# Issuing the loads of x for four pairs of chunks from GpSimd instead of SyncE, in a fused Mamba-2 and SwiGLU kernel

## The chip, the core and the metric

The kernel runs on one core of one Trainium2 chip. The core has five engines that run their own instruction streams: TensorE (PE in the profile, with its weight loads listed apart as PEld), VectorE (DVE), ScalarE (ACT), GpSimd (POOL) and SyncE (SP). SP does no arithmetic; it issues transfers between DRAM and the on-chip memory (DMAs). Sixteen DMA engines carry them out. An engine works through its own stream in order, so an instruction that waits holds up everything behind it on that engine.

The metric is the time of one execution on the device in microseconds. The kernel before takes 395.5 us, the median of 3 runs (395.0 to 396.29).

## The reference

Two stages follow one another. The first is a Mamba-2 scan in chunks, for 4 batches of 8 heads, 768 positions, a head width of 32 and a state of 16:

```python
for c in range(nc):
    la = log_a[:, :, sl]
    cum = np.cumsum(la, axis=-1)
    L = np.exp(cum[:, :, :, None] - cum[:, :, None, :]) * causal
    CB = np.einsum('bhin,bhjn->bhij', Cc, Bc)
    y_intra = np.einsum('bhij,bhjd->bhid', CB * L, xc)
    y_inter = np.einsum('bhin,bhnd->bhid', Cc, state) * np.exp(cum)[:, :, :, None]
    y[:, :, sl] = y_intra + y_inter
    Bx = np.einsum('bhjn,bhjd->bhjnd', Bc, xc) * decay_from_j[:, :, :, None, None]
    state = decay_full[:, :, None, None] * state + np.sum(Bx, axis=2)
```

The second takes the result as 3072 tokens of 256 features, divides each by its root mean square, and applies a SwiGLU layer with a hidden width of 1536:

```python
xn = x / rms * rms_g
g = xn @ w_gate
silu = g * (1.0 / (1.0 + np.exp(-g)))
val = xn @ w_val
out = silu * val @ w_out
```

x enters the scan in two places: as the factor of the masked matrix in `y_intra`, and in the additions to the state, `Bx`.

## The kernel before, in words

The kernel works on chunks of 128 positions, taken in twelve pairs: pair p holds chunks 2p and 2p + 1 of one batch. Two pairs make one block of 512 tokens for the second stage, so there are six blocks. The pairs are counted from 0 in what follows, so the third to sixth pairs are pairs 2 to 5. Blocks 1 to 5 compute the products with the gate and value weights (`product_gv`, L917 to L936, step `P.k.j`) by a scheme that needs seven products instead of eight for each 2 by 2 arrangement of submatrices; it works on sums and differences of weights, which `combine_w` (L893 to L904, steps `cw` on DVE and `cwp` on POOL) makes once, and of activations, which `combine_x` (L906 to L912, steps `tx` on DVE and `txp` on POOL) makes for each block. Block 0 uses it for the last three of its six columns, and plain products for the others (`products_gv` L849, `products_early` L859).

Before they can be used, the weights pass through a conversion: `fetch` (L153) loads a piece of a weight matrix into one of six buffers `wr`, `power` (ACT, L199), `mantissa` (DVE, L216 and L219) and `weight` (DVE, L225) turn it into the wanted numbers. This fills the first 95 us of DVE and ACT.

No scheduler decides the order. A string of steps at the end of the kernel is read from left to right, and each step emits its instructions on the engines that its function names. A word such as `0:x.2` calls the function that is listed under `x` in `first_kinds` for pair 2; the steps of the blocks 1 to 5 are looked up in `kinds` instead. The order of each engine's stream is thus the order of the words. Waits are put in for data and for buffers. A DMA is issued in the stream of the engine whose queue is named, at its place in that stream.

The loads of x are made by `load_x(p, queue)` (L127 to L132). It takes one of the three buffers `xr` and issues two DMAs, one for each chunk, each with 128 positions on the partitions and, for each position, 8 heads of 32 numbers: 1024 runs of 128 bytes, 128 KB. The step `x` in `settings` (L373) serves pairs 0 to 5, and the step `x` in `kinds` (L1247) serves pairs 6 to 11. With three buffers, pair 2 takes a fresh one, pairs 3 and 5 those of pairs 0 and 1, and pair 4 that of pair 2.

Around the four loads the order reads (cut, with only the words that are spoken of below):

```
0:sq.0 ... 0:y.1/2 0:sq.1 ... 0:xn.0 ... 0:dT.3 0:man.4 0:table.1 0:x.2 ... 0:gate.2/0 0:txp.0.0 0:cw.0.0
0:gg.2/1 ... 0:A.2 0:txp.0.1 0:silu.3 0:x.3 ... 0:tx.0.2 1:dT.0 1:table 0:txp.0.3 ... 0:cwp.3.0 ... 0:cw.4.0
... 0:y.2/2 0:S.3 0:x.5 0:cwp.4.1 ... 0:P.2.3 0:bc.4 0:x.4 ... 0:sq.2 ... 0:cwp.3.3 0:P.5.3 1:spread.0 0:cwp.1.0
0:P.7.3 0:P.6.4 0:P.5.4 0:P.4.3 0:hidgp.11.3 ... 0:cwp.4.2 0:cwp.4.3 ... 0:P.3.3 ... 0:cwp.5.0 ... 0:P.7.4 ... 0:y.3/2
```

The takers of x are: `A.2` (L648), the additions to the state for pair 2; `y.2` (L720), the outputs of pair 2, at whose end stand the additions for pair 3; and `y.3`, the outputs of pair 3, at whose end stand the additions for pairs 4 and 5. On POOL in this stretch are `sq` (L761 and L772, sums of squares), `txp`, `cwp` (written as `sw<-...` and `wgv<-wgv` in the profile, since one of the four combinations is made in place) and `hidgp` (L960, the product of the two halves of the hidden layer).

Of the kernel before, what the change touches and what calls it, by code (L numbers as in the profile page):

```python
# [20 lines left out]
def kernel(  # L21
# [33 lines left out]
    nc = tc.nc  # L55
# [71 lines left out]
    def load_x(p, queue=nc.sync):  # L127
        b, c0 = divmod(2 * p, NC)
        st.setdefault(p, {})["x"] = raw.tile([P, 2, NH, D], FP32, tag="xr", name="xr")
        for i in range(2):  # L130
            sl = slice((c0 + i) * P, (c0 + i + 1) * P)
            queue.dma_start(out=st[p]["x"][:, i], in_=x[b, :, sl, :].rearrange("h s n -> s h n"))  # L132
# [210 lines left out]
    def minus_mid():  # L343
# [26 lines left out]
        "log": lambda: activation(out=la, in_=la0, func=AF.Ln), "mids": minus_mid,  # L370
        "bc": lambda p: load(p, (nc.sync, nc.scalar) if p == 0 else (nc.sync,) * (1 if p == 1 else 2)),
        "bc2": load_chunk,
        "x": load_x,  # L373
    }


# [1082 lines left out]
```

## Time and profile before

| | |
|---|---|
| median of 3 runs | 395.5 us (395.0 to 396.29) |
| the profiled execution's own time | 395.41 us |
| its span, from the first to the last instruction | 393.7 us |
| granted TensorE clock | 1.00 |
| busy: PE, PEld | 386.9, 332.2 us |
| busy: DVE, ACT, POOL | 285.3, 234.1, 151.8 us |
| DMA: packets, of them under 512 bytes | 92533, 77416 |
| DMA: bytes moved | 27.01 MB |

The profile is of one execution, whose own time stands beside its span. Times in its rows are microseconds from the start of the span. A row of the order of time gives the start, the length, the engine, the line of the kernel, the operation, what it writes and reads, and how many instructions are merged into the row; brackets show how long the engine was idle before and what it waited for. SPq is SP's queue: its rows are the issues, not the transfers themselves. A transfer's landing is given as the time from its issue. Matmuls are pipelined and their ends are modelled, so that PE can show as busy without being at its peak. The DMA engines' share is the mean over all 16.

### The profile page before, as it was taken

To read this page: it belongs to the slowest core of one execution; us is meant where nothing else is said; L and a number is where in the kernel's file an instruction comes from. 1 tells how busy PE (TensorE), PEld (TensorE's weight loads), DVE (VectorE), ACT (ScalarE), POOL (GpSimd) and SP (SyncE) were. 2 spreads that over 40 slices of the span, in tenths; PEclk is the share of its full clock that TensorE was granted. 3 is DMA by queue.
4 is the path that set the end of the run, shared out by engine and by line. 5 is a ranking of instruction groups with operands and counts; after the bars stand their busy time and mean duration, and the time that the engine had idled before them with its cause. 6 is when DMAs were issued, how large, how long until landed. Compare 5 with 4: busy or idle time off the path is not lost.

```text
span 393.7 us, 9631 instructions
## 1 busy us (share of the span) xinstructions
PE 386.9 (98%) x3837; PEld 332.2 (84%) x3837; DVE 285.3 (72%) x594; ACT 234.1 (59%) x483; POOL 151.8 (39%) x170
## 2 busy tenths in 40 slices
PE   8999999999999999999999999999999999999996
PEld 5675478888888899888889888899888899988995
DVE  7999999997748967484897765676654587455574
ACT  3899889978599492447651544676345740555410
POOL 5022054454648378003563611466402155211271
PEclk9999999999999999999999999999999999999999
DMA  8988986682002538202423002000100000100001
GB/s 93 252 173 249 246 153 210 121 160 63 6 0 68 78 85 128 70 0 36 102 44 75 15 0 68 2 23 28 43 0 3 0 8 27 55 0 2 1 2 53
DMA packets 92533, 27.01 MB, mean 69 GB/s; under 512 B 77416, under 2 KB 86344, under 8 KB 92488
## 3 DMA queue, kind: packets, MB, share of 16 engines
q1 hardware_dynamic: 90408, 26.26, 29.8%
q8 instruction: 30, 0.49, 0.5%
q10 hardware_dynamic: 2080, 0.13, 0.4%
q14 instruction: 15, 0.12, 0.1%
HBM read 22.64 MB, written 3.74 MB: 67 GB/s over the span
## 4 chain that ended last, share of the span: by engine, by line
PE 81%; DVE 11%; issue 4%; ACT 3%; DVEq 0%; ACTq 0%
PE gate L935 27%; PE o L1056 21%; PE val L935 20%; PE o L967 4%; PE y L720 3%; PE g L583 1%; DVE wgv L225 1%; DVE m L219 1%; DVE m L216 1%; PE tp L533 1%; DVE hid L882 1%; PE g L576 1%; PE e L453 1%; PE y L648 1%; DVE S L672 1%
## 5 line engine op out<-in xcount | busy, mean ns | idle before, releaser
L947 DVE TENSOR_TENSOR c<-val,p 128x512 f32<-128x512 f32 x99 | 67.5, 687 | 40.3 <-PE val L935 28.3
L941 ACT COPY p<-gate 128x512 f32<-128x512 f32 x99 | 56.9, 584 | 58.0 <-PE gate L935 56.3
L960 POOL TENSOR_TENSOR hid<-c 128x256 f32<-128x256 f32 x41 | 34.0, 837 | 88.8 <-ACT c L197 82.6
L935 PE MATMUL gate<-tx,wgv 128*128 128x256 f32 x264 | 65.8, 382 | 0.0
L197 ACT ACTIVATE c<-c 128x256 f32<-128x256 f32 x99 | 39.3, 415 | 30.1 <-DVE c L947 29.6
L935 PEld LDWEIGHTS gate<-tx,wgv 128*128 128x128 f32 x264 | 49.0, 190 | 7.2 <-issue 0.3
L960 DVE TENSOR_TENSOR hid<-c 128x256 f32<-128x256 f32 x58 | 28.4, 498 | 17.0 <-ACT c L197 17.0
L1087 DVE TENSOR_TENSOR ob<-ob,o 128x128 f32<-128x128 f32 (+1 forms) x90 | 24.4, 299 | 20.7 <-PE o L1056 18.0
L1056 PE MATMUL o<-two,hid 128*128 128x128 f32 x280 | 36.2, 276 | 0.1
L1056 PEld LDWEIGHTS o<-two,hid 128*128 128x128 f32 x280 | 34.4, 192 | 1.1 <-issue 0.2
L935 PE MATMUL val<-tx,sw 128*128 128x256 f32 x132 | 34.0, 382 | 0.0
L935 PE MATMUL val<-xn,sw 128*128 128x256 f32 x132 | 33.7, 380 | 0.0
L935 PE MATMUL gate<-tx,sw 128*128 128x256 f32 x132 | 33.4, 381 | 0.0
L935 PE MATMUL gate<-xn,wgv 128*128 128x256 f32 x132 | 33.2, 381 | 0.2 <-DVE xn L831 0.2
L935 PE MATMUL val<-xn,wgv 128*128 128x256 f32 x132 | 33.3, 380 | 0.0
L486 POOL TENSOR_SCALAR_AFFINE_SELECT L<-L 64x512 f32<-64x512 f32 x32 | 23.0, 718 | 13.5 <-ACT L L197 10.9
L935 PEld LDWEIGHTS val<-tx,sw 128*128 128x128 f32 x132 | 24.7, 190 | 4.0 <-issue 0.4
L935 PEld LDWEIGHTS val<-xn,wgv 128*128 128x128 f32 x132 | 24.9, 190 | 3.4
L935 PEld LDWEIGHTS gate<-xn,wgv 128*128 128x128 f32 x132 | 24.4, 190 | 4.0 <-ACT e L197 0.6
L935 PEld LDWEIGHTS gate<-tx,sw 128*128 128x128 f32 x132 | 24.6, 190 | 3.4 <-issue 0.2
L197 ACT ACTIVATE u<-gate 128x256 f32<-128x256 f32 (+1 forms) x37 | 14.8, 402 | 21.2 <-PE gate L935 20.1
L935 PEld LDWEIGHTS val<-xn,sw 128*128 128x128 f32 x132 | 24.5, 190 | 3.2 <-issue 0.2
(199 smaller groups left out, 737.2 us busy)
## 6 DMA issues: line engine op xcount, KB each, us to landing
L<-rowd SPq DMA_DIRECT2D x32, 128.0 KB, 3.3
xr<-in_x_dram SPq DMA_DIRECT2D x24, 128.0 KB, 3.8
wr<-in_moe_w_out_dram SPq DMA_DIRECT2D x6, 512.0 KB, 3.6
out_dram<-ob SPq DMA_DIRECT2D x24, 128.0 KB, 1.7
wr<-in_moe_w_gate_dram SPq DMA_DIRECT2D x5, 512.0 KB, 6.3
wr<-in_moe_w_val_dram SPq DMA_DIRECT2D x5, 512.0 KB, 4.9
br<-in_B_dram SPq DMA_DIRECT2D x23, 64.0 KB, 2.9
cr<-in_C_dram SPq DMA_DIRECT2D x23, 64.0 KB, 2.9
```

Source lines behind the costliest of these rows:

```text
L197: nc.scalar.activation(**operands)
L216: nc.vector.tensor_scalar(out=m, in0=hi, scalar1=0xFFFFF, scalar2=0x100000, op0=ALU.bitwise_and, op1=ALU.bitwise_or)
L219: nc.vector.scalar_tensor_tensor(out=f, in0=lo.bitcast(U32), scalar=2.0 ** -32, in1=m, op0=ALU.mult, op1=ALU.add)
L486: nc.gpsimd.affine_select(out=L[r], in_=L[r], pattern=[[0, L.shape[1]], [1, HC]], compare_op=ALU.is_ge, fill=0.0, base=0, channel_multipli ...
L720: nc.tensor.matmul(out=y[2 * k + u][rows, (2 * n + i) * HC:(2 * n + i + 1) * HC], start=(k, u, rows.start) not in opened, stop=True, skip_ ...
L935: nc.tensor.matmul(out=dst[:, half[w]], lhsT=lhsT, rhs=rhs, start=(k in (1, 2, 5) and w == 0), stop=True, skip_group_check=True)
L941: nc.scalar.copy(out=t, in_=Xs[j])
L947: nc.vector.tensor_tensor(out=t, in0=Zs[j], in1=a, op=ALU.add)
L960: engine.tensor_tensor(out=hid[:, 2 * j + c // 10 - 1, c % 10 - 1], in0=u, in1=src[:, half[1]], op=ALU.mult)
L967: nc.tensor.matmul(out=o, lhsT=hid[:, f, k // 2, (k % 2) * P:(k % 2 + 1) * P], rhs=wo[:, f], start=opens, stop=(f == NF - 1), skip_group_c ...
L1056: nc.tensor.matmul(out=Os[blk, b][:, place * P:(place + 1) * P], lhsT=hidden_or_sum(u)[:, g], rhs=rhs, start=(blk, b) not in opened, stop= ...
L1087: nc.vector.tensor_tensor(out=o, in0=o, in1=src, op=ALU.add if what[0] == "+" else ALU.subtract)
```

## The change

The step `x` for the pairs 0 to 5 names the queue itself: SP for pairs 0 and 1, GpSimd for pairs 2, 3, 5 and 4, in this order. The words in the order string stay where they are. `load_x` is unchanged, and so is the step `x` of the later blocks.

```diff
-        "x": load_x,
+        "x": lambda p: load_x(p, nc.sync if p < 2 else nc.gpsimd),
```

By the order of the words, the eight issues leave SP's stream and enter POOL's: those of pair 2 stand between the second `sq` of L761 and `txp.0.0`, those of pair 3 between `txp.0.1` and `txp.0.3`, those of pair 5 between `cwp.3.0` and `cwp.4.1`, and those of pair 4 between `cwp.4.1` and the `sq` of pair 2. The streams of PE, DVE and ACT hold the same instructions in the same order. The waits of the eight DMAs on their buffers move with them.

## Prediction

> **What bounds the kernel now.** I read the page's totals and chain first, then the queue that the loads leave and the one they enter, then who takes what stands behind them.
>
> From the page: the busy times, the chain of work that ended last, and the loads in question.
>
> ```profile
> PE 386.9 (98%) x3837; PEld 332.2 (84%) x3837; DVE 285.3 (72%) x594; ACT 234.1 (59%) x483; POOL 151.8 (39%) x170
> ...
> PE 81%; DVE 11%; issue 4%; ACT 3%; DVEq 0%; ACTq 0%
> ...
> xr<-in_x_dram SPq DMA_DIRECT2D x24, 128.0 KB, 3.8
> ```
>
> PE is busy 386.9 of 393.7 us, so at most 6.8 us are left to win in the whole span, while whatever makes PE wait is added to the end. The granted clock is 1.00 in every stretch.
>
> The order of time on SP's queue shows the four pairs of loads as they go out now (start, length of the two):
>
> ```profile
> 32.34 1.08 SPq L132 DMA_DIRECT2D xr<-in_x_dram  x2
> ...
> 35.49 2.26 SPq L132 DMA_DIRECT2D xr<-in_x_dram  x2
> ...
> 48.97 2.09 SPq L132 DMA_DIRECT2D xr<-in_x_dram  x2
> ...
> 54.59 2.26 SPq L132 DMA_DIRECT2D xr<-in_x_dram  x2
> ```
>
> They are pairs 2, 3, 5 and 4 (counted from 0). Now POOL's own order of time; brackets give the idle time before and what ended it:
>
> ```profile
> 30.85 0.73 POOL L912 TENSOR_TENSOR tx<-xn 128x256 f32<-128x256 f32 x1 [7.51 <-DVE xn L835]
> 31.66 1.59 POOL L912 TENSOR_TENSOR tx<-xn,tx 128x256 f32<-128x256 f32 x2
> 49.68 1.12 POOL L904 TENSOR_TENSOR sw<-wgv 128x256 f32<-128x256 f32 x1 [16.43 <-DVE wgv L225]
> 52.95 0.73 POOL L904 TENSOR_TENSOR sw<-sw,wgv 128x256 f32<-128x256 f32 x1 [2.15 <-DVE sw L904]
> 55.10 0.73 POOL L772 TENSOR_TENSOR sq<-sq 128x256 f32<-128x256 f32 x1 [1.42 <-ACT sq L197]
> 55.79 0.74 POOL L904 TENSOR_TENSOR sw<-wgv,sw 128x256 f32<-128x256 f32 x1
> 56.48 0.74 POOL L904 TENSOR_TENSOR sw<-wgv 128x256 f32<-128x256 f32 x1
> 57.19 1.18 POOL L960 TENSOR_TENSOR hid<-c 128x256 f32<-128x256 f32 x1
> 58.33 0.90 POOL L904 TENSOR_TENSOR wgv<-wgv 128x256 f32<-128x256 f32 x1
> 59.20 0.73 POOL L904 TENSOR_TENSOR sw<-wgv,sw 128x256 f32<-128x256 f32 x1
> 62.23 0.87 POOL L904 TENSOR_TENSOR sw<-wgv 128x256 f32<-128x256 f32 x1 [2.29 <-DVE wgv L225]
> ```
>
> Two wide holes (7.51 and 16.43 us), two narrow ones (2.15 and 1.42), then a run without a gap from 55.10 to 59.93. What this run makes are weights for PE, and PE's weight loads say when each is taken:
>
> ```profile
> 57.32 0.84 PEld L935 LDWEIGHTS gate<-tx,sw 128*128 128x128 f32 x4
> ...
> 59.91 0.84 PEld L935 LDWEIGHTS val<-xn,sw 128*128 128x128 f32 x4
> 60.77 0.84 PEld L935 LDWEIGHTS gate<-tx,wgv 128*128 128x128 f32 x4
> ```
>
> The chain in order of time is PE alone from 55.08 to 63.79: a wait there is paid in full.
>
> **The change part by part.**
>
> *Taken from SP.* Eight issues, 1.08 + 2.26 + 2.09 + 2.26 = 7.7 us of its queue. The loads behind them (gate and value weights, dT, B and C, the rows for L) may go out up to that much sooner. I cost this at nothing: the weight loads wait for their buffers (SP waited 1.7 us for ACT's e and 3.9 us for DVE's m), and their takers do not wait: between 20 and 60 us DVE is 97% busy and its longest idle piece is 0.24 us. If that cover were gone, the gain would be bounded by PE's idle time between 50 and 60 us, 0.51 us.
>
> *Added to POOL.* Eight issues of 128 KB, each of 128 x 8 runs of 128 bytes. In program order pair 2 stands behind the second sq of L761 (done at 23.34), pair 3 between the second and third tx, pair 5 behind the first sw (50.80), pair 4 behind the second (53.68). Only pair 4 has a late release: it takes pair 2's buffer when y.2 is over at 49.9, so it does not wait either. Everything on POOL behind an issue waits for it.
>
> The trace has no DMA issued by POOL, so the price g of one issue is bounded. Below: SP's issue of the same load, 0.37 us at its shortest, 0.58 at the median. Above: one step of POOL's own two-input operation for every run, 731 ns / 256 = 2.85 ns, times 1024 = 2.9 us; with a step for each of the two ends of a run, 5.8 us. Between lies POOL's one-input operation, the affine select of L486, 718 ns / 512 = 1.40 ns a step: 1.44 us. I take this one, the nearest to work that reads no operands, plus the 0.58 of an issue: **g = 2.0 us**. It is an estimate.
>
> Pair 2 then holds POOL from 23.4 to 27.4, inside the 7.51 us hole. Pair 3 holds it from 32.4 to 36.4, inside the 16.43; the third tx behind it is wanted by PE at 59 us. Both are hidden up to g = 3.7. Their data come in time: pair 3 is wanted at 49.3 by the additions in y.2, and SP's pairs landed at most 6.9 us after issue.
>
> Pair 5: 50.80 to 54.80 (the hole of 2.15 covers half); the second sw ends at 54.80 + 0.73 = 55.53 instead of 53.68, and PE takes it at 57.32: hidden. Pair 4: 55.53 to 59.53. The sq that started at 55.10 now starts at 59.53, so the run is D = 4g - 3.57 = 4.4 us late. Its products:
> - sw<-wgv,sw ends at 56.53 and is taken at 59.91: slack 3.4, so PE waits 1.0.
> - wgv<-wgv ends at 59.23 and is taken at 60.77: slack 1.5, so PE waits 4.4 - 1.5 = 2.9 in all (the 1.0 is in it).
> - hid of L960 ends at 58.37; its buffer is wanted again at 66.54: hidden.
> - the next sw waits for DVE at 62.23: 2.29 us of idle take up half of the lateness and PE's own delay the rest.
>
> Pair 4 lands at 59.53 + 3.8 = 63.3, and is wanted at 62.99 plus PE's 2.9. The term is **+2.9 us**, between 0 (g at most 1.3) and 18 (g = 5.8).
>
> *DMA traffic moved.* Pair 2 comes 9 us earlier. Its 2048 packets are small: 2439 packets under 512 B filled 67.5% of 54.5 to 57 us, 1.7 us of all 16 engines, so pair 2 takes 1.4. Between 24 and 32 us the engines are busy 1.03, 0.83, 1.02 and 0.88 of each 2 us, and 0.39 in the next. The nearest taker behind is DVE's T of L557 at 31.89, whose dT was issued at 26.71; at the 4.5 us of its neighbours that lands at 31.2, 0.7 before. Bounds 0 and 1.4 - 0.7 = 0.7; shared in turn, half of 1.4 meets the slack, so I take 0.
>
> **Sum.** 395.41 for the profiled execution (span 393.7 and 1.7 around it) + 2.9 = **398.3 us**. That execution lies 0.1 below the median of 395.5.
>
> **A rule against the change.** The trace shows POOL and DVE slowing one another: POOL's 128x256 operation takes 0.73 us alone and 1.12 at 49.68 with DVE busy, and DVE's copy of L670 took 0.55 at 53.18 beside POOL, 0.20 at 18.15 without. The Trainium skill, page "SBUF — State Buffer", section "SBUF: two separate sides", its box on DMAs issued from GpSimd, says that VectorE in a two-port mode locks GpSimd out of the port that it writes descriptors through, and names 620 ns alone against 3100 ns beside a VectorE copy. Put in for g, that page's 3.1 us would give D = 8.8 and 402.7. On the other side the page "DMA: Bandwidth & Descriptors", section "Anatomy of one DMA", calls descriptor generation small, with many emitted before the cost shows; by that g stays near 1 and the sum is 395.4. No row of this trace shows either.
>
> **The rivals.**
> - *Hidden.* If g is at most 1.3, the two narrow holes and the 1.5 us of slack take all of it; up to 1.6, PE loses 1.3 at most. For: SP's 0.58 us. Against: POOL has no row that handles 1024 pieces in less than 1.4. 394.9 to 396.7; the lower end is the 0.51 of PE's idle time.
> - *Stretched.* DVE is busy 9.62 of the 10 us from 50 on; with POOL's own stretch of 1.12 / 0.73 = 1.5, g = 2.0 becomes 3.1, D = 8.8, PE waits 7.3: 402.7. Against: between 55.1 and 57 POOL's rows kept 0.73.
> - *Slow issue.* A step for both ends, g = 5.8: pair 3 would be sent by 48.2 and land after 49.3; D = 19.6 and PE waits 18: 413.
> - *Early traffic.* dT lands 0.7 late, DVE hands that on, nothing else: 396.1, inside the measurement.
> - *SP freed.* For a gain of more than 1.2 us the earlier loads would have to end waits of PE beyond 60 us, in which no load is named: below 394.3.
>
> **How the numbers follow.** A difference of 0.3%, 1.2 us, is about what a measurement can tell. Forecast, g from 1.6 to 2.6: 0.33 (own range 396.7 to 400.8). Stretched, up to 406: 0.20. Slow issue, beyond: 0.11. Hidden, with early traffic: 0.28. SP freed: 0.08. Slower 0.64, same 0.28, faster 0.08. The range leaves out the slow issue and the freed SP, 0.19: 394.5 to 406.
>
> **What would show it.** Right: POOL's sq of L772, now at 55.10, starts 3 to 6 us later; PE's weight load from wgv, now at 60.77, waits for POOL; nothing moves before 59 us, and the shift found there is still there at the end. Wrong: the run from sq on starts within 1.5 us of its time (hidden); DVE waits at 31.9 (traffic); the tx at 30.85 late or y.2 waiting for xr at 49.3 (g above 3.7); DVE's rows longer around 24, 34 and 52 us, which I have priced at nothing.

## The result, and the profile after

The changed kernel takes **400.28 us** (median of 4 runs, 399.69 to 401.89), the kernel before 395.51 (4 runs, 395.0 to 396.29): a ratio of 1.0125, 95% interval 1.009 to 1.016. It is slower by 4.8 us. The forecast said 398.3, slower, within 394.5 to 406. The direction and the range hold; the mechanism that was forecast does not, as the profile shows: GpSimd's issues are cheap and nothing of PE's waits for GpSimd, while two other places, priced at nothing, cost the time. The profiled execution took 401.89 us, with a span of 400.2 against 393.7: the 6.5 us that are accounted for below are of this execution, which lies 1.6 above the median.

From the page of the changed kernel, the totals, the queues, the chain of work that ended last and the loads that stayed on SP:

```profile
PE 389.0 (97%) x3837; PEld 333.2 (83%) x3837; DVE 287.1 (72%) x594; ACT 234.4 (59%) x483; POOL 158.9 (40%) x178
...
q0 software_dynamic: 384, 1.05, 1.3%
...
PE 83%; ACT 6%; DVE 5%; DMA 3%; issue 3%; DVEq 0%; ACTq 0%; SPq 0%
...
xr<-in_x_dram SPq DMA_DIRECT2D x16, 128.0 KB, 3.4
```

The change did what it says: a new queue, q0, carries 1.05 MB, the eight loads of 128 KB. DMA now has a share of 3% in the chain, in which before it had none. The order of time on POOL has the new issues, and the run of weight steps behind them:

```profile
23.98 2.01 POOL L132 DMA_DIRECT2D xr<-in_x_dram  x2
...
33.03 1.96 POOL L132 DMA_DIRECT2D xr<-in_x_dram  x2
...
54.64 1.78 POOL L132 DMA_DIRECT2D xr<-in_x_dram  x2
...
58.25 1.78 POOL L132 DMA_DIRECT2D xr<-in_x_dram  x2
60.05 0.74 POOL L772 TENSOR_TENSOR sq<-sq 128x256 f32<-128x256 f32 x1
60.73 0.74 POOL L904 TENSOR_TENSOR sw<-wgv,sw 128x256 f32<-128x256 f32 x1
61.42 0.72 POOL L904 TENSOR_TENSOR sw<-wgv 128x256 f32<-128x256 f32 x1
62.11 0.71 POOL L960 TENSOR_TENSOR hid<-c 128x256 f32<-128x256 f32 x1
62.80 0.71 POOL L904 TENSOR_TENSOR wgv<-wgv 128x256 f32<-128x256 f32 x1
63.48 0.72 POOL L904 TENSOR_TENSOR sw<-wgv,sw 128x256 f32<-128x256 f32 x1
```

A pair of issues takes 1.8 to 2.0 us, so one takes about 0.9, not the 2.0 of the forecast. The sq of L772 did start 4.95 us later (60.05 against 55.10), as was forecast to show the mechanism right. It is a trap: DVE, which does not depend on these issues, is nearly as late at that place. Its wgv of L225 starts at 61.37 against 56.74, 4.63 later. POOL's own lateness is the difference, 0.3 us.

PE's waits between 20 and 75 us, of the kernel before and then of the changed one (us in total, times, longest):

```profile
PE g L583 <- ACT sq L197: 0.5, 1, 0.5
```
```profile
PE g L583 <- DVE T L557: 3.2, 1, 3.2
PE val L935 <- DVE c L947: 1.6, 1, 1.6
```

Neither wait is for POOL. The first begins some 20 us ahead of the place where the forecast looked.

**Place one: T waits for dT.** In the changed kernel SP's order of time, and the two T of DVE, read:

```profile
25.21 0.68 SPq L1145 DMA_DIRECT2D rowe<-e_sb  x1
...
29.85 0.66 SPq L551 DMA_DIRECT2D dT<-rowe  x1
...
33.85 0.62 SPq L551 DMA_DIRECT2D dT<-rowe  x1
```
```profile
33.76 0.42 DVE L557 TENSOR_TENSOR T<-tp,dT 128x256 f32<-128x256 f32 x1 [1.09 <-DMA dT<-rowe]
...
39.86 0.42 DVE L557 TENSOR_TENSOR T<-tp,dT 128x256 f32<-128x256 f32 x1 [2.09 <-DMA dT<-rowe]
```

The same rows of the kernel before:

```profile
23.73 0.71 SPq L1145 DMA_DIRECT2D rowe<-e_sb  x1
...
26.71 0.65 SPq L551 DMA_DIRECT2D dT<-rowe  x1
...
31.67 0.62 SPq L551 DMA_DIRECT2D dT<-rowe  x1
```
```profile
31.89 0.42 DVE L557 TENSOR_TENSOR T<-tp,dT 128x256 f32<-128x256 f32 x1
...
35.97 0.42 DVE L557 TENSOR_TENSOR T<-tp,dT 128x256 f32<-128x256 f32 x1
```

rowe holds the decays of the scan as rows in DRAM; dT reads them back, spread over the partitions. So SP holds the issue of dT until rowe has landed (the waits of SP's queue name it, 2.9 us for the first dT against 1.2 before), and everything behind it on SP's queue waits too. With pair 2 on its way from 23.98, the first dT follows rowe after 4.64 us instead of 2.98. The DMA engines had no room for pair 2 at that time. In the kernel before, the windows and the queue's own row read (start and end, length, busy time of PE, PEld, DVE, ACT and POOL, granted clock, DMA share, GB/s; and packets, MB, share of 16 engines from 24 to 26 us):

```profile
24.00:26.00 2.00, 2.00 (x9) 1.37 (x9) 1.96 (x6) 1.94 (x4) 0.00 (x0) 1.00 1.03 108
```
```profile
q1 hardware_dynamic: 2240, 0.22, 102.5%
```

The 1.03 is a share: all 16 engines were busy throughout, and the three windows behind it show 0.83, 1.02 and 0.88. The prediction took these four numbers for microseconds out of 2, that is, for engines half free.

Not all of the first wait is the change's. rowe itself went out 1.48 us later than in the profile before, and the loads ahead of it on SP were 1.2 us late already when pair 2 was issued. In the two runs with memsets described below, which have no early pair, rowe went out as late (25.55 and 25.29), and there the first T waited 2.00 and 1.83 us.

The second dT, issued at 33.85 just behind pair 3's issue at 33.03, reaches its T at 39.86, 6.0 us later; before, the T at 35.97 followed its issue by 4.3 and had no wait. This second wait is not a matter of the late issue: in the two memset runs the second dT went out at 33.76 and 33.40 without pair 3 under way, and its T ran at 37.48 and 37.32 with no wait. The second T reads the PSUM tile `tp`, whose place the next product g takes: that is PE's wait of 3.2 us. The chain in order of time has exactly these pieces:

```profile
30.61 3.19 DMA rowe<-e_sb
...
33.85 5.92 DMA dT<-rowe
...
39.86 0.44 DVE T L557
...
40.34 0.65 PE g L583 x20
41.00 8.76 PE gate L849 x16
```

**Place two: the clock.** The last row is 1.7 us longer than the same 16 products before, which ran from 37.03 to 44.09. PE's weight loads behind the wait, with the idle time before them, and then the windows from 38 us on, with columns as above (the granted clock was 1.00 in all of these in the kernel before):

```profile
40.34 0.41 PEld L583 LDWEIGHTS g<-T 32*64 32x64 f32 x20 [3.48 <-DVE T L557]
```

```profile
38.00:40.00 2.00, 0.00 (x0) 0.00 (x0) 0.14 (x1) 0.86 (x2) 0.00 (x0) 1.00 1.03 306
40.00:42.00 2.00, 1.66 (x22) 1.05 (x23) 2.00 (x5) 0.60 (x1) 0.00 (x0) 0.86 1.05 375
42.00:44.00 2.00, 2.00 (x3) 0.67 (x2) 1.93 (x4) 1.90 (x3) 0.00 (x0) 0.50 0.85 238
44.00:46.00 2.00, 2.00 (x5) 0.91 (x4) 1.97 (x5) 1.93 (x4) 0.00 (x0) 0.79 0.22 77
```

PE's weight loads sat idle for 3.48 us; then four products of the gate ran at a spacing of 0.85 us instead of 0.43, which is the 1.7 us. The Trainium skill, page "TensorE: Matmul & The Clock Gate", section "What's actually happening", says that an idle window of about 3.4 us halves the clock and that a busy one of the same length restores it. This trace agrees: 3.48 us of idle time, a granted clock of 0.50, four slow products in 3.4 us. Other runs here differ from the idle window: 2.53 us of idle time halved the clock as well (the last run below), while 2.19 us (pair 3 alone) did not. In this kernel, then, the drop has been seen from 2.5 us of idle time on.

**Place three: DVE's wgv.** The row of DVE, in the changed kernel and in the kernel before:

```profile
61.37 3.38 DVE L225 SCALAR_TENSOR_TENSOR wgv<-m,e 128x512 f32<-128x512 f32 x1
```
```profile
56.74 1.03 DVE L225 SCALAR_TENSOR_TENSOR wgv<-m,e 128x512 f32<-128x512 f32 x1
```

The same operation took 0.69 us at 61.45 of the kernel before. Here it takes 3.38 and ends at 64.75, half a microsecond after POOL's run without a gap (60.05 to 64.20). The c of L947 behind it on DVE is late, PE's val waits 1.6 us for that, and PE's weight load for val<-xn,sw comes at 66.46 instead of 59.91.

So the account of the profiled execution: at wgv the kernel is 4.63 us late, namely about 0.7 that the execution was already behind at 20 us, ahead of every changed instruction (the first sq of L761 on POOL starts at 20.28 instead of 19.59), which is scatter between executions; 3.2 from PE's wait for T; 1.7 from the clock; less about 1.0 that slack gave back (0.5 of it is PE's wait for ACT's sq, which is gone). The wait behind wgv makes 66.46 - 59.91 = 6.55 of it, and that is the 6.5 of the span.

### The profile page after: what moved, and what is told of

Read it like the earlier page. It is cut to its first block, busy times and chain, and to the rows that moved or that the text cites. A ratio compares the mean times of both kernels' runs of the same rounds, so it can differ in the third digit from the quotient of the medians.

```text
span 400.2 us, 9638 instructions
## 1 busy us (share of the span) xinstructions
PE 389.0 (97%) x3837; PEld 333.2 (83%) x3837; DVE 287.1 (72%) x594; ACT 234.4 (59%) x483; POOL 158.9 (40%) x178
## 2 busy tenths in 40 slices
DMA packets 84597, 27.01 MB, mean 67 GB/s; under 512 B 69224, under 2 KB 78152, under 8 KB 84552
## 3 DMA queue, kind: packets, MB, share of 16 engines
q1 hardware_dynamic: 82088, 25.21, 28.3%
q0 software_dynamic: 384, 1.05, 1.3%
HBM read 22.64 MB, written 3.74 MB: 66 GB/s over the span
## 4 chain that ended last, share of the span: by engine, by line
PE 83%; ACT 6%; DVE 5%; DMA 3%; issue 3%; DVEq 0%; ACTq 0%; SPq 0%
PE gate L935 26%; PE o L1056 21%; PE val L935 20%; PE o L967 3%; PE gate L849 3%; PE y L720 3%; ACT e L197 2%; DMA dT<-rowe 1%; PE g L583 1%; DVE wgv L225 1%; ACT sq L197 1%; PE tp L533 1%; DMA rowe<-e_sb 1%; PE g L576 1%; PE y L648 1%
## 5 line engine op out<-in xcount | busy, mean ns | idle before, releaser
L947 DVE TENSOR_TENSOR c<-val,p 128x512 f32<-128x512 f32 x99 | 67.5, 687 | 40.4 <-PE val L935 28.4
L197 ACT ACTIVATE u<-gate 128x256 f32<-128x256 f32 (+1 forms) x37 | 14.8, 403 | 24.3 <-PE gate L935 20.1
```

The source lines that it names most:

```text
L197: nc.scalar.activation(**operands)
L947: nc.vector.tensor_tensor(out=t, in0=Zs[j], in1=a, op=ALU.add)
```

## The experiments

Every time below is a median, compared with the kernel before as run on the same chip. That one took 395.37 us (31 runs) for pair 2 alone, pair 3 alone, pairs 5 and 4 alone, and pair 2 early on SP; 395.91 (29) for pair 2 behind dT, the two runs with late pairs and the memsets at both places; 395.68 (23) for dT ahead of fetch.7, the memsets at x.4 alone, the shifted run and the last run.

### Which pair costs what

The changed line is made for one pair or two alone; the other loads stay on SP.

```diff
+        "x": lambda p: load_x(p, nc.gpsimd if p == 2 else nc.sync),
```

> Only the loads of pair 2 are issued by GpSimd. Traffic theory (pair 2's data go out 8 us early in a queue of their own, hold up rowe and dT, DVE's T of L557 comes late, and PE waits in g of L583): the T rows wait for DMA dT, PE waits 1 to 3.5 us in g near 40 us, time 396.5 to 399. Theory of the forecast (POOL's run of weights after 55 us is late): nothing stands behind pair 2 on POOL until 30 us, so 395.5, no wait in g. Port theory (DVE's wgv of L225 near 61 us blocked by POOL's gapless run): 395.5, no long wgv row, since pairs 5 and 4 are back on SP.

Measured: 397.32 us (396.4 to 399.48), ratio 1.0041, 1.0011 to 1.0072. In its profile the first T waits 1.20 us for dT, PE's g 0.8; wgv takes 1.02; the clock stays at 1.00.

```diff
+        "x": lambda p: load_x(p, nc.gpsimd if p == 3 else nc.sync),
```

> Only the loads of pair 3 are issued by GpSimd, near 32.4 us. Traffic theory: dT of pair 3 is in flight at the time, from 31.7 to at most 36.0, and shares the engines with packets of 4096 bytes; the second T row comes up to 1.5 us late, PE waits up to 1 us in g; 395.5 to 396.7. If all of the loss near 40 us comes from pair 3 and none from pair 2: 398 or more. Theory of the forecast and port theory: 395.5.

Measured: 396.29 us (395.63 to 398.0), ratio 1.0028, 0.9999 to 1.0056: by itself this one can't be told from no change. Its profile does show the place: the second T waits 1.54 us for dT, PE's g 1.9. After that shorter wait (PE's weight loads idle for 2.19 us) the clock stays at 1.00.

```diff
+        "x": lambda p: load_x(p, nc.gpsimd if p in (4, 5) else nc.sync),
```

> Only the loads of pairs 5 and 4 are issued by GpSimd. Traffic theory alone: no change near 40 us, 395.5. Theory of the forecast with the measured issue of 0.9 us: the sq row at 55.10 starts at most 0.4 us later, and no weight of POOL's is late, 395.5. Port theory: POOL's run from 55 on is without holes, DVE's wgv row of L225 near 57 us takes 2 to 3.4 us instead of 1.03, c of L947 follows late, PE waits about 2 us in val of L935 near 60 us; 397 to 398.

Measured: 397.97 us (397.44 to 398.36), ratio 1.0051, 1.0024 to 1.0077. Both T are without a wait. DVE and POOL at the third place, and PE's wait:

```profile
56.81 3.39 DVE L225 SCALAR_TENSOR_TENSOR wgv<-m,e 128x512 f32<-128x512 f32 x1
```
```profile
53.69 1.78 POOL L132 DMA_DIRECT2D xr<-in_x_dram  x2
55.48 0.74 POOL L772 TENSOR_TENSOR sq<-sq 128x256 f32<-128x256 f32 x1
56.17 0.74 POOL L904 TENSOR_TENSOR sw<-wgv,sw 128x256 f32<-128x256 f32 x1
56.86 0.73 POOL L904 TENSOR_TENSOR sw<-wgv 128x256 f32<-128x256 f32 x1
```
```profile
PE val L935 <- DVE c L947: 1.6, 1, 1.6
```

POOL's sq is 0.38 us late, and that costs nothing: PE waits for DVE. So the two places are independent, early pairs at T and late pairs at wgv. The excesses 1.95, 0.92 and 2.60 sum to 5.5 against the 4.8 of the whole change. The sum isn't expected to be exact, since waits that follow one another share slack and the clock's loss comes by steps (below).

### The early traffic, without GpSimd

If the cost at T comes from pair 2 being under way early, it must appear with every load on SP too.

```diff
-        0:g.1.0/2 0:exp.1.0 0:L.1.0 0:fetch.4 0:last.0
+        0:g.1.0/2 0:exp.1.0 0:L.1.0 0:x.2 0:fetch.4 0:last.0
...
-        0:early.1.1 0:dT.3 0:man.4 0:table.1 0:x.2 0:norm.1
+        0:early.1.1 0:dT.3 0:man.4 0:table.1 0:norm.1
```

> All loads stay on SP, but pair 2 goes out in front of the weights of fetch.4, at 24.5 instead of 32.3 us, which is where GpSimd sent it. If early bytes by themselves do the harm, dT comes late as with GpSimd: rowe's landing is not held up, as rowe goes out before, but dT stands behind 2048 more packets, up to 1.4 us; 396 to 397.5. If it is the other queue with its packets of 4096 bytes, which takes its turn ahead of small packets: T waits less than 0.7 us, 395.5.

Measured: 399.73 us (396.67 to 400.51), ratio 1.0087, 1.0056 to 1.0119. The first T and the clock:

```profile
35.11 0.42 DVE L557 TENSOR_TENSOR T<-tp,dT 128x256 f32<-128x256 f32 x1 [3.51 <-DMA dT<-rowe]
```
```profile
40.00:42.00 2.00, 2.00 (x6) 0.84 (x3) 1.93 (x5) 1.93 (x4) 0.00 (x0) 0.50 0.98 289
```

The wait for dT and the slow clock come without any issue on GpSimd: it is enough that pair 2 goes out early. The queue is not indifferent, though. On SP, ahead of the weights, the early pair costs 4.4 us, more than either branch expected and more than twice the 1.95 from GpSimd; why was not taken apart.

```diff
-        ... 0:fetch.7 0:dT.2 0:tok 0:tokout
+        ... 0:fetch.7 0:dT.2 0:x.2 0:tok 0:tokout
```

(and x.2 taken from its old place, as above: pair 2 on SP directly behind the first dT)

> All loads on SP; pair 2 goes out right behind dT of pair 2, near 27.3 us, instead of ahead of the weights in front of it (399.7) or at 32.3 (before). Traffic theory: what stands behind pays. The first T row no longer waits for its dT (3.5 us with pair 2 in front); the second rowe, wr and dT come up to 1.5 us later, so the second T row may wait up to 1 us: 395.4 to 397. If early bytes hurt wherever they stand in the queue: 398 or more.

Measured: 396.85 us (395.98 to 400.85, two runs of ten at 400.8), ratio 1.0044, 1.0014 to 1.0074. In the profile the first T has no wait, PE's g waits 0.9. Behind the first dT, the pair no longer delays that dT, and most of the cost is gone, not all.

```diff
-        0:last.0 0:Tl.0 0:fetch.7 0:dT.2 0:tok
+        0:last.0 0:Tl.0 0:dT.2 0:fetch.7 0:tok
```

> The kernel before with SyncE's fetch.7 behind dT.2. In the runs of before the first T now and then waits for dT. If the order on SyncE's queue sets when dT lands: dT.2 issued earlier, T of DVE with no wait, 395.0 to 395.6 us, with fewer of the longer runs. If rowe's own landing sets it, no change: 395.4 to 395.9 us. A loss (396 or more) only if the weights of fetch.7 are then late.

Measured: 396.9 us (395.51 to 398.72), ratio 1.0028, 1.0008 to 1.0048: slower, not better. dT follows rowe by 2.95 us, as before (2.98): what holds dT is rowe's landing, not the weights ahead of it on the queue. Where the loss comes from was not seen; the profiled execution, at 395.88, is one of the three shortest.

Over the profiles the time from the first rowe to the first dT sorts itself. With pair 2 sent before or with rowe: 3.43 us (pair 2 on SP early), 3.46 and 3.74, and 4.64 in the changed kernel. In the ten others: 2.81 to 3.07. Likewise the second T waits for dT in three profiles, 1.52 to 2.09 us: the three kernels in which GpSimd issues pair 3 at 32.9 to 33.0, ahead of the second dT. The first T is less clean: it waits 1.0 to 2.0 us in three profiles in which nothing before 33 us was changed. There rowe was issued at 24.3 to 25.6 instead of 23.7: the slack of this dT is thin in the kernel before as well. In the changed kernel's profile rowe was late too, at 25.21, so its first wait can't be put to pair 2 by that profile alone. That pair 2 costs time is shown by the medians of the runs that move it, and by the longer way from rowe to dT.

The clock joins in by steps. By an estimate from the 3.4 us at half clock seen above, one such stretch lowers the mean granted clock of an execution of 395 us from 1.00 to 0.996, and two lower it to 0.991. Counted over all executions, a mean of 0.996 or less is called a drop here:

| kernel | executions with a drop | median with, without |
|---|---|---|
| before (three sets) | 5 of 83 | 397.63, 395.61 |
| changed | 4 of 4 | 400.28, none |
| pair 2 alone on GpSimd | 3 of 10 | 398.37, 396.81 |
| pair 3 alone | 3 of 10 | 397.87, 396.05 |
| pair 2 early on SP | 9 of 10 | 399.78, 396.67 (one) |
| pair 2 on SP behind dT | 4 of 10 | 399.46, 396.63 |
| pairs 5 and 4 alone | 1 of 10 | 397.44 (one), 397.98 |
| dT ahead of fetch.7 | 3 of 10 | 397.83, 396.59 |

So the early pairs cost in two ways: some 0.7 to 1.4 us in executions without a drop, and drops made frequent. Executions with one are longer by 1.6 us and up, the longer wait that goes with it included. The kernel before has the same drop now and then, and the late pairs don't add to it. The run with dT ahead of fetch.7 has 3 in 10 without any early pair, so an early pair may not be the only thing that brings it.

### The late pairs: lateness, phase or the issues themselves

Here pairs 2 and 3 are issued by GpSimd, but at 37.85, held back by a one-element copy that waits for a result of DVE (their words x.2 and x.3, and the two txp, are moved there); pairs 5 and 4 stay at the places of the change.

```diff
+        "gate0": lambda: nc.gpsimd.tensor_copy(out=held_back, in_=Sw[0][:, 0, 0, 0:1]),
...
-        0:gate.2/0 0:txp.0.0 0:cw.0.0 0:gg.2/1
+        0:gate.2/0 0:txp.0.0 0:cw.0.0 0:txp.0.1 0:txp.0.3 0:gate0 0:x.2 0:x.3 0:gg.2/1
```

> All four pairs are issued by GpSimd, but pairs 2 and 3 only when POOL has copied one element of what DVE's first sw writes, near 37 us, so after both dT have landed. Traffic theory: no T row waits for dT, PE does not wait in g near 36 to 40 us, the granted clock stays at 1.00 there, and what is left is the loss of pairs 5 and 4: 397.5 to 398.3, the time of the run with these two alone (397.97). If issuing by GpSimd costs by itself wherever it stands: 400, as the change.

Measured: 397.47 us (396.87 to 398.43), ratio 1.0041, 1.0027 to 1.0054. The clock is 1.00, wgv takes 3.35 us, PE's val waits 1.5. The cost at T is down to a g wait of 0.7, though the first T still waits 1.01; the cost at wgv is whole. The late start has a price of its own: PE's additions for pair 2 wait 0.7 us for xr. Next, x.5 is taken along to the early place, so that only pair 4 is issued ahead of the run:

```diff
-        0:txp.0.3 0:gate0 0:x.2 0:x.3 0:gg.2/1
+        0:txp.0.3 0:gate0 0:x.2 0:x.3 0:x.5 0:gg.2/1
...
-        0:y.2/2 0:S.3 0:x.5 0:cwp.4.1
+        0:y.2/2 0:S.3 0:cwp.4.1
```

> As the run before, and pair 5 follows pair 3 in POOL's hole near 41 us; only pair 4 is left between POOL's weights. Port theory: POOL's run from 55 on is at most 0.4 us late. If its start relative to DVE's wgv decides, wgv of L225 near 57 us takes 1.0 again and PE does not wait in val: 395.2 to 396.0, no slower than before with all four pairs on GpSimd. If any DMA ahead of the run is enough: wgv 3.4 us and 397.5 to 398.3.

Measured: 396.9 us, ratio 1.0026, 1.001 to 1.0043, in two groups of five runs: 395.84 to 396.34, and 397.46 to 397.87. The profiled execution is of the first group and has wgv at 1.03 us and no wait of val; PE's additions for pair 2 wait 1.5 us for xr in it. That wgv is long in the second group would fit the size of the step, 1.5 us, but no trace shows it, and a later xr could do the same.

Now POOL is held as long without any load: every load on SP, and memsets of POOL at the places of x.5 and x.4.

```diff
+        "hold": lambda n: [nc.gpsimd.memset(chunk_ones, 0.0) for k in range(n)],
...
+        0:x.5 0:hold.6 0:cwp.4.1 ... 0:bc.4 0:x.4 0:hold.6 0:switch.0
```

> No load is issued by GpSimd. POOL instead writes zeros six times into a tile that is no longer read, about 2 us, in each of the two places where pairs 5 and 4 were issued. If it is the lateness of POOL's run that blocks DVE: wgv of L225 near 57 us takes 2 to 3.4 us, PE waits in val, 397 to 398.3. If the issue of a DMA by GpSimd itself is needed (descriptors): wgv about 1.0, 395.2 to 396.

Measured: 395.79 us (395.14 to 397.05), ratio 0.9995, 0.9983 to 1.0008: no cost, though POOL is held 2.2 to 2.3 us at each place, longer than by a pair of issues. wgv takes 0.97. Against DVE's wgv, POOL's run starts 0.6 us later than in the kernel before, twice the 0.3 of the change. That ends the theory that POOL's lateness is what costs here: at this size the slack takes it. The 4.4 us of the forecast were never reached.

Looking at these profiles I formed a theory of phase: wgv is held through the whole run when it starts just ahead of one of POOL's steps. Three runs were made for it. The first puts POOL's run where the issues put it, by memsets at x.4 alone:

```diff
+        0:bc.4 0:x.4 0:hold.5 0:switch.0
```

> The kernel before, every load on SyncE, with five memsets of 0.36 us each on GpSimd at the place of x.4: 1.8 us, the length of the pair of load issues there, with no transfer behind them, so that GpSimd's run of weight steps should start near 55.48, where it starts when pairs 4 and 5 are issued by GpSimd. Theory of phase (the place at which GpSimd's gapless run stands to DVE's wgv of L225 decides; what held GpSimd is no matter): wgv lasts about 3.4 us, PE's val waits 1.6 us for c, 397 to 398 us. Rival (the load issues themselves, or their transfers, hold DVE up): wgv lasts 0.7 to 1.1 us, no wait, 395.0 to 395.9 us.

Measured: 395.99 us (395.15 to 397.21), ratio 1.0008, 0.9993 to 1.0024. DVE and POOL:

```profile
58.08 0.68 DVE L225 SCALAR_TENSOR_TENSOR wgv<-m,e 128x512 f32<-128x512 f32 x1
```
```profile
54.95 1.83 POOL L1211 MEMSET chunk_ones<- 128x256 f32 x5
56.75 0.73 POOL L772 TENSOR_TENSOR sq<-sq 128x256 f32<-128x256 f32 x1
...
58.13 1.23 POOL L904 TENSOR_TENSOR sw<-wgv 128x256 f32<-128x256 f32 x1
```

wgv starts 0.05 us ahead of the sw, exactly as with pairs 4 and 5 on GpSimd (56.81 and 56.86). There DVE was held for 3.39 us; here DVE runs at once and POOL's step is the longer one, 1.23. The second run shifts the phase and keeps the issues:

```diff
+        "x": lambda p: load_x(p, nc.gpsimd if p in (4, 5) else nc.sync),
...
+        0:bc.4 0:x.4 0:hold.1 0:switch.0
```

> Pairs 4 and 5 on GpSimd, as in the run that gave 397.97 us, with one more memset of 0.36 us behind x.4's issues: GpSimd's run starts later by half of one of its steps (0.7 us). Theory of phase: wgv of L225 then starts some 0.3 us behind the start of a GpSimd step instead of just ahead of one, lasts about 1.0 us, and the time falls to 395.2 to 396.3 us although GpSimd is later. Rival (GpSimd's lateness itself costs the time): 398.0 to 398.5 us. Rival (the transfers that GpSimd issues cost it): 398 us, unchanged.

Measured: 398.01 us (397.29 to 399.71), ratio 1.0063, 1.0044 to 1.0083.

```profile
56.38 3.63 DVE L225 SCALAR_TENSOR_TENSOR wgv<-m,e 128x512 f32<-128x512 f32 x1
```
```profile
55.99 0.74 POOL L904 TENSOR_TENSOR sw<-wgv,sw 128x256 f32<-128x256 f32 x1
```

wgv now starts 0.39 us behind the start of a step and is held all the same. The theory of phase falls twice: same phase, other result; other phase, same result. What sorts the profiles is whether GpSimd issued both late pairs shortly before its run: wgv takes 3.35 to 3.63 us in the five that did, and 0.68 to 1.03 in the nine that did not.

The last run put both ideas into the changed kernel, dT.2 ahead of fetch.7 and one memset behind x.4:

```diff
-        0:last.0 0:Tl.0 0:fetch.7 0:dT.2 0:tok
+        0:last.0 0:Tl.0 0:dT.2 0:fetch.7 0:tok
...
+        0:bc.4 0:x.4 0:hold.1 0:switch.0
```

> The changed kernel with both causes met: the weights' load fetch.7 stands behind dT.2 on SyncE, so that dT.2 has a shorter queue before it, and one memset of 0.36 us stands on GpSimd behind x.4's issues. All four pairs are still issued by GpSimd at the places of the change. If the three causes (dT late, the clock that falls after PE's long idle, the phase of wgv) are the whole cost: 395.5 to 397.3 us. If one of them is not met by its edit, its part stays: 398 to 399 us with dT still late, 397.3 to 398.5 with wgv still at 3.4 us. The forecast's reading (GpSimd's lateness alone) gives 400.3 us or more.

Measured: 400.7 us (398.35 to 401.93), ratio 1.0106, 1.0056 to 1.0157. Nothing is won, as follows from the two runs above. The first T has no wait in this profile, but the second still waits 1.52 us, and wgv takes 3.63. PE's waits, the idle time of its weight loads, and the clock behind it:

```profile
PE g L583 <- DVE T L557: 2.3, 1, 2.3
PE val L935 <- DVE c L947: 1.8, 1, 1.8
```
```profile
39.26 0.58 PEld L583 LDWEIGHTS g<-T 32*64 32x64 f32 x20 [2.53 <-DVE T L557]
```
```profile
40.00:42.00 2.00, 2.00 (x6) 0.84 (x3) 1.93 (x5) 1.94 (x4) 0.00 (x0) 0.50 1.06 376
```

No version tried beats the kernel before.

## Why the prediction was right or wrong

- **Slower, and by how much.** Right in sign, 2.0 us short in size, inside the range. It is right for the wrong reason: of the time lost, none comes from GpSimd's lateness, where the +2.9 was put. That the size came within 2.0 us is luck.
- **g = 2.0 us for one issue.** Mis-sized. It measures 0.88 to 1.12 us, median 0.90. I had taken the nearest operation that handles 1024 pieces one by one; GpSimd's queue moved 1.05 MB in 384 packets, so the 1024 runs do not become packets of their own there. With 4 x 0.9 - 3.57 the lateness D is near 0, and 0.3 to 0.4 was measured. The rival "hidden" was right about POOL. The rule of the Trainium skill, page "DMA: Bandwidth & Descriptors", section "Anatomy of one DMA", that descriptor generation is small, was the better one of the two.
- **The run late, PE waits 2.9 for its weights.** Failed with g: in the profile after, PE never waits for POOL. The run with memsets shows that even 2.3 us at each place is free.
- **"DMA traffic moved ... I take 0" (bounds 0 and 0.7).** This step failed most. It began with a misreading: 1.03, 0.83, 1.02 and 0.88 are shares of all 16 engines, not microseconds of each 2, so between 24 and 32 us the engines were nearly full and pair 2's 1.4 us could only come in ahead of something else. Pair 2 does go out some 8 us earlier, and DVE's T is the nearest taker, but the step followed one dT from its issue to its landing. It left out that the issue itself waits for rowe's landing, which came later with pair 2 under way; that a second dT meets pair 3; that T frees the place in PSUM that PE's g needs; and that a long idle time of PE (3.48 us here) brings the clock down. The two T waited 1.09 and 2.09 instead of at most 0.7 for one, which became 3.2 for PE and 1.7 more by the clock; the 1.09 a late rowe can make by itself, the 2.09 was seen only with pair 3 under way. The rival "early traffic" named the place and stopped at "nothing else".
- **"DVE's rows longer around 24, 34 and 52 us, which I have priced at nothing."** The right kind of cost at another place: one row, at 61.37, longer by 2.35, and about 1.9 us at PE's val.
- **A rule against the change, and the rival "stretched".** They expected GpSimd's issues to be held by DVE. The issues were not: 0.9 us each beside a busy DVE (1.97 of the 2 us from 24 us on). It went the other way, DVE held by GpSimd. The Trainium skill, page "SBUF — State Buffer", section "SBUF: two separate sides", calls the pair of ports that the two engines share an exclusive lock, given to whichever instruction starts first, for the whole of that instruction. The traces agree that one of the two runs at its usual length while the other is held (POOL's sw 1.23 beside wgv 0.68, wgv 3.39 beside POOL's 0.7), but not with the order: in the held runs DVE waits through four or five of POOL's steps, most of which started after wgv. The 620 and 3100 ns that the prediction took from the same section of the Trainium skill are there the times of a whole DMA, not of its issue, so putting 3.1 us in for g took the one for the other.
- **Taken from SP, a gain of nothing.** Right: no wait that the freed queue could have ended shows up, and no version is faster.
- **What would show it.** "The sq of L772 3 to 6 us later" came true through another cause. "Nothing moves before 59 us" did not hold, and "DVE waits at 31.9 (traffic)", named as a sign of being wrong, came (1.09 us, at 33.76). A row that is late says where the delay has arrived, not where it began; the neighbours' lateness has to be taken off first.

Open: why issuing both late pairs on GpSimd lets its next steps hold DVE off, while memsets of the same length do not. It could be the issues' effect on how GpSimd queues its next instructions, or the transfers themselves; no run separates them. Open too: where the run with dT ahead of fetch.7 loses its 1.2 us.

## What to carry to other kernels

A load that moves to an idle engine's queue also moves in time: before pricing the issue, list every transfer that it will now travel beside, and follow each to its taker through the writes that the taker's load waits for. A stall of PE costs more than its length once the clock comes down with it, and the mean granted clock of each execution tells which ones paid that. And test a suspected engine by holding it with harmless work of the same length: here that took the suspicion off GpSimd's lateness in one run.

## What was not expected of the hardware

- One issue of 1024 runs of 128 bytes took GpSimd 0.88 to 1.12 us; the same load took SP 0.37 at its shortest and 0.58 at the median (longest 1.79). The packets under 512 bytes fell from 77416 to 69224, by 8 x 1024, while the bytes stayed at 27.01 MB.
- After 3.48 us of idle time of its weight loads PE's clock was granted at half for about 3.4 us, and so it was after 2.53 us; after 1.08 and 2.19 us, in the profiles with pair 2 or pair 3 moved alone, it was not. Over all executions the mean clock lies mostly near 1.00, 0.996 or 0.991, and 5 of 83 executions of the kernel before have such a drop too.
- An operation of DVE of 0.69 us took 3.35 to 3.63 us beside a run of POOL without gaps, in all five profiles in which GpSimd had just issued two pairs of loads, and in none of the other nine.
